# Weight preparation inside the first block of an MLP: bursts against single operations at five places of a round

## The chip, the cores and the metric

The kernel runs on one core of one Trainium2 chip. The metric is the device time of one execution in microseconds (us); lower is better. Five engines matter: PE (TensorE, matmuls), DVE (VectorE), ACT (ScalarE), POOL (GpSimd, nearly unused here) and SP, which issues all DMAs from one queue, in order.

## The reference, cut to what matters

Attention with two kinds of mask gives 2304 tokens of 512 values. Two MLPs follow, one after the other, each with its own `w_in` (512 x 2048) and `w_out` (2048 x 512):

```python
x = attention(q, k, v)                      # 2304 x 512
h = x @ w1_in;  x = relu(h)**2 @ w1_out     # first MLP
h = x @ w2_in;  g = h * sigmoid(1.702 * h)  # second MLP
out = g @ w2_out
```

The inputs are 64-bit floats. Only the preparation of `w2_out`, late in the kernel, is touched here.

## The kernel before, in words

**Number format.** A 64-bit weight is decoded to a 32-bit one by integer operations (`decode_ops`, L140 to L160), and each 32-bit operand is then split into a rounded part and a rest (`wh`, `wl`), so that each product is made of several matmuls.

**The second MLP multiplies by Strassen's scheme.** Each pair of 128-wide slices of the hidden dimension is a pair `p` (0 to 7), and for each pair and each of the two weight matrices seven combinations of the quarter matrices are prepared once, and written to the DRAM tiles `w2d` and `wo2d`. `decode2(o, p)` (L564 to L600) is a Python generator that prepares one pair: an absolute value on ACT (L571), four integer operations on DVE (L146, L148, L153, L157), the sums and differences of quarters on DVE (L582; three for `w_out`), the rounding on ACT (L594, 1792 columns), the rest on DVE (L596, 1792 columns), and two stores of 896 KB on SP (L599). Between any two of these it yields, so that the caller decides where in the instruction order each operation goes. `fill(dve, act)` (L752) draws operations until a budget of estimated microseconds on DVE or ACT is used up. A step may also yield nothing: a pair is begun only two steps of the counter `now` after its raw weights were fetched, and its rounding only two steps after the pair before was finished. Most of the 16 preparations are drawn during the first MLP; at the start of the second MLP the last two pairs of `w_out` (pairs 6 and 7) remain. They are staged in the free tiles `misc[3]` (`wh`) and `misc[4]` (`wl`), where the earlier ones used `wst`.

**The block of the second MLP.** There are three blocks (`i`) of 768 tokens, each with eight rounds (`p`), one for each pair, and then an output stage (L1037 on). A round does seven products (`product`, L669, six matmuls at L673 each) in this order on PE: product 2, product 3, product 6 of the round before, product 4, products 0 and 1 of the next round, product 5. Product 5 adds to the bank X, so it waits until ACT has copied X away (`s3`, L853). On ACT this copy stands behind a sigmoid of the round before (L453), which waits for a DVE addition of the round before (`add`, L845, in `rest`, L994). DVE also multiplies by the sigmoids (L456) and in odd rounds from 3 on forms two sums (`sums`, L866, L848). The order on PE, DVE and ACT is the order of the program (`manual_schedule`); the order of SP's DMAs is made by the planner, which puts a DMA where it expects its operands to be ready, often far ahead of its place in the program. A product's weights are fetched two rounds ahead, into the buffer that the product of this round has just left (`stream`, L656).

**Where the remaining work is drawn.** In rounds 0 to 4 of block 0, `fill(1.8, 1.8)` stands between the DVE multiplication L955 and the addition of `rest`; in round 5, `fill(99, 99)` drains what is left. Then `stream_out(0)` (L875) asks for the first output weights: one load of 1 MB into `misc[5]` for pairs 0 to 3, and one for each of pairs 4 to 7. In round 7 `stream_out(1)` asks for the second set. Each output step `mm_out` (L896) is 18 matmuls at L904.

Of the kernel before, what the change touches and what calls it, by code (L numbers as in the profile page):

```python
# [10 lines left out]
F32R = mybir.dt.float32r  # L11
# [11 lines left out]
def kernel(  # L23
# [20 lines left out]
    nc = tc.nc  # L44
# [519 lines left out]
    def decode2(o, p):  # L564
        while (o, p) not in raw or now[0] < raw[o, p][1] + 2:
            yield None
        place, _ = raw.pop((o, p))
        s, t = stages[place], tmp()
        t2 = t[:, 0:4].rearrange("p x n -> p (x n)")
        s = s.rearrange("p x n -> p (x n)").bitcast(I32).rearrange("p (n two) -> p n two", two=2)  # L570
        nc.scalar.activation(t2, s[:, :, 1].bitcast(F32), AF.Abs)  # L571
        yield "A", 1.06
        for c, _ in zip((0.7, 0.7, 1.2, 1.2), decode_ops(s, t2, False)):
            yield "D", c
        fetch2(place)
        if o:

            forms = ((slice(4, 7, 2), slice(1, 4, 2), slice(0, 2)), (5, 3, 4), (1, 2, 5))
        else:
            forms = ((5, 0, 2), (2, 2, 3), (4, 2, 0), (6, 1, 4))  # L580
        for to, a, b in forms:
            nc.vector.tensor_tensor(  # L582
                out=t[:, to], in0=t[:, a], in1=t[:, b], op=ALU.add if (o, to) == (0, 2) else ALU.subtract)
            yield "D", 0.69 if isinstance(to, slice) else 0.43
        while late and not misc:
            yield None
        if late:
            wh, wl = (misc[n][:, 0:7 * 2 * P].bitcast(F32R).rearrange("p (j n) -> p j n", j=7) for n in (3, 4))
        else:
            w = wstage()  # L590
            wh, wl = w[:, :, 0], w[:, :, 1]
        while now[0] < now[1] + 2:
            yield None
        nc.scalar.copy(wh, t)  # L594
        yield "A", 1.68
        nc.vector.tensor_tensor(out=wl, in0=t, in1=f32(wh), op=ALU.subtract)  # L596
        yield "D", 1.97
        for x, w in enumerate((wh, wl)):
            nc.sync.dma_start(wo2d[:, :, p, x] if o else w2d[:, p, :, x], f32(w))  # L599
        now[1] = now[0]  # L600
# [271 lines left out]
    JS = ((0, "X"), (1, "Z"), (0, "X"), (2, "Y"), (4, "X"), (1, "Y"), (3, "X"))  # L872
    LAST = 4 * len(JS) - 1

    def stream_out(j):  # L875
        if j % 2 == 0:
            src = wo2d[:, WOSEL[j], 0:4].rearrange("p a h n -> p (a h n)")
            nc.sync.dma_start(f32(misc[5]), src)
        for p in range(4 if j % 2 == 0 else 0, NP):
            src, (w, *parts) = wo2d[:, WOSEL[j], p], wx[j % 2][p]  # L880
            if w is not None:
                nc.sync.dma_start(f32(w), src)
            else:
                for h, w in enumerate(parts):
                    nc.sync.dma_start(f32(w), src[:, h])

    def makeop(q):
        j, c = divmod(q, 4)
# [52 lines left out]
    for i in range(N2):  # L941

        waiting, third = iter(()), lambda: None
        for p in range(NP):
            n, c, x = i * NP + p, p // 2, p % 2
            now[0] += 1
            product(n, 2, X, start=False)
            next(waiting, None)
            add(s1, Z[:, 0:NH])
            t = sig(s1, "gh")  # L950
            next(waiting, None)
            s2 = copied(X, 2 + p % 2)
            Y = bank("h")
            product(n, 3, Y)
            times(gf[c][0][:, x], s1, t)  # L955
            if c and x:
                sums(gf[c - 1])
            if i == 0 and p < 6:
                fill(*(1.8, 1.8) if p < 5 else (99, 99))
            if p == 5:  # L960
                stream_out(0)
            if p > 5:
                makeop(p - 6)
            third()
            if p + 1 == NP:
                stream_out(1)
            product(n, 4, X, start=False)
            next(waiting, None)
            s3 = copied(X, 4)
            if p + 1 < NP:  # L970
                Xn = first(n + 1)
                Z = bank("acc")
                product(n + 1, 1, Z)
            else:
                Zo, Xo = ([bank("acc") for _ in range(2)] for _ in range(2))
                mm_out(0, Xo)
            add(s3, Y[:, 0:NH])
            if p + 1 < NP:
                s1 = copied(Xn, (p + 1) % 2)
            next(waiting, None)  # L980
            t = sig(s3, "gh")
            times(gf[c][3][:, x], s3, t)
            product(n, 5, X, start=False)
            def third(n=n, Y=Y):
                product(n, 6, Y, start=False)

            def rest(c=c, x=x, s2=s2, X=X, Y=Y):
                g = gf[c]
                t = lpool.tile([P, NH], F32, tag="tx", name="tx", bufs=1)
                sigmoid(X[:, 0:NH], t)  # L990
                yield
                times(g[1][:, x], X[:, 0:NH], t)
                yield
                add(s2, Y[:, 0:NH])  # L994
                t = sig(s2, "gh")
                yield
                times(g[2][:, x], s2, t)

            waiting = rest()
            X = Xn  # L1000


        more = i + 1 < N2
        if more:
            raw_x = wstage().rearrange("p j h n -> p (j h n)")[:, 0:KC * 2 * NH]
            wst.clear()
            extra = make_x(load_raw(i + 1, f32(raw_x).rearrange("p (c n) -> p c n", c=KC)))
        st = ring(2, [2, 3, 2 * P], F32, "so")
        st2 = tmp()[:, 0:6].rearrange("p (a m) n -> p a m n", a=2)
        ps = {"X": Xo, "Z": Zo, "Y": None}  # L1010
        next(waiting)
        next(waiting)
        makeop(2)
        mm_out(1, Xo)
        third()

        def evac(j):
            if j == 0:
                moved(ps["X"], st[:, 0], nc.scalar.copy)
            elif j == 1:  # L1020
                moved(ps["Z"], st[:, 0], add)
                store(i, 0, 0, st[:, 0])
            elif j == 2:
                moved(ps["X"], st2[:, 0], nc.scalar.copy)
            elif j == 3:
                moved(ps["Y"], st[:, 1], nc.scalar.copy)
            elif j == 4:
                moved(ps["X"], st[:, 1], add)
                store(i, 1, 1, st[:, 1])
            elif j == 5:  # L1030
                moved(ps["Y"], st2[:, 0], add)
                store(i, 0, 1, st2[:, 0])
            else:
                moved(ps["X"], st2[:, 1], nc.scalar.copy)
                store(i, 1, 0, st2[:, 1])

        for q in range(1, LAST + 1):  # L1037
            j, c = divmod(q, 4)
            if q < LAST - 1:
                makeop(q + 2)  # L1040
            if q == 12:
                ps["Y"] = [bank("h") for _ in range(2)]
            if q == LAST and more:
                X = first((i + 1) * NP)
            if q > 1 and (q < LAST or more):
                mm_out(q, ps[JS[j][1]])
            if c == 0:
                evac(j - 1)
            if q == 1:
                next(waiting, None)  # L1050
                next(waiting, None)
            if q == 2:
                sums(gf[3])
            if 3 <= q < 7:
                g = gf[q - 3]
                sub2(g[0], g[2], g[0])
            elif q > 6:
                next(extra, None)
                if q in (9, 11, 13, 15):
                    g = gf[(q - 9) // 2]  # L1060
                    sub2(g[1], g[1], g[0])
            if c == 3 and j + 2 < len(JS):
                stream_out(j + 2)
            if q == 24 and more:
                for _ in extra:
                    pass
                stream((i + 1) * NP)
                stream((i + 1) * NP + 1)
        if more:
            Z = bank("acc")  # L1070
            product((i + 1) * NP, 1, Z)
            hs = ring(2, [5, NH], F32, "hs")
            s1 = copied(X, 0)
            evac(6)
        else:
            mm_out(LAST, ps["X"], (2,))
            nc.vector.tensor_copy(st2[:, 1, 2], ps["X"][1][:, 0:2 * P])
            store(i, 1, 0, st2[:, 1], slice(2, 3))
            mm_out(LAST, ps["X"], (0, 1))
            nc.scalar.copy(st2[:, 1, 0], ps["X"][0][:, 0:2 * P])  # L1080
            nc.vector.tensor_copy(st2[:, 1, 1], ps["X"][0][:, 2 * P:4 * P])
            store(i, 1, 0, st2[:, 1], slice(0, 2))
# [45 lines left out]
```

## Time and profile before

| | us |
|---|---|
| median of 3 runs (884.33 to 886.2) | 884.43 |
| the profiled execution, its own time | 884.62 |
| its span in the trace | 882.8 |
| start of product 4 of round 0 to the first output matmul, block 0 (516.33 to 577.66) | 61.33 |
| the same stretch of block 1 (644.36 to 696.88) | 52.52 |

The profile is of one execution, and every time in it counts from the start of the span. The profiled execution's time is 1.82 us more than its span (what lies around the span), and 0.19 us above the median. Engine times overlap, so busy shares don't add up. A row of the timeline merges neighbouring instructions of one kind: start, length, engine, line, operation, tiles written and read, shape, count, and in brackets the idle time before it with the engine and line that ended it. A product of six matmuls takes 1.05 us from its start to that of the next; the last matmul's modelled end lies some 0.16 us behind that.

### The profile page before, as it was taken

The page shows a single profiled execution, that of the slowest core. Times are in us where ns is not written, and L with a number is a line of the kernel's source. Part 1 is how long each engine was busy: PE and PEld are TensorE (multiplying, and loading weights), DVE is VectorE, ACT ScalarE, POOL GpSimd, SP SyncE. Part 2 cuts the span into 40 slices and gives each one's busy share as a digit, 9 for nine tenths or more (in the row PEclk, how much of TensorE's full clock was granted, in tenths as well). Part 3 has the DMA queues.
Part 4 walks back from the last instruction along what each step waited for, and adds up shares of the span by engine and source line. Part 5 has one row for each costly group of instructions (what it writes and reads, how often), then busy time and mean ns, then how long its engine had stood idle before and what let it go on. Part 6 is the DMA issues. An engine that isn't in the chain of part 4 may idle for free.

```text
span 882.8 us, 15997 instructions
## 1 busy us (share of the span) xinstructions
PE 863.1 (98%) x5851; PEld 771.0 (87%) x5857; DVE 613.9 (70%) x1315; ACT 492.7 (56%) x1160; POOL 2.6 (0%) x12
## 2 busy tenths in 40 slices
PE   8899999999999999999999998899999999999998
PEld 5578788888889998888877898899999999999998
DVE  5999996545546645788868767688646798357863
ACT  7988895544536645555646644455444555344542
POOL 0000000000000000000000000000000000000000
PEclk9999999999999999999999999999999999999999
DMA  8997210211114205887999499978898497986673
GB/s 203 302 324 227 65 34 28 88 39 47 34 34 113 46 2 188 267 266 267 311 334 297 136 334 368 310 258 280 271 371 251 161 340 258 334 286 206 200 249 109
DMA packets 146129, 181.85 MB, mean 206 GB/s; under 512 B 41508, under 2 KB 101124, under 8 KB 144516
## 3 DMA queue, kind: packets, MB, share of 16 engines
q1 hardware_dynamic: 146052, 180.84, 62.7%
q8 instruction: 47, 0.77, 0.4%
q14 instruction: 30, 0.25, 0.1%
HBM read 142.00 MB, written 38.80 MB: 205 GB/s over the span
## 4 chain that ended last, share of the span: by engine, by line
PE 68%; DVE 16%; ACT 6%; issue 4%; DMA 3%; SPq 1%; ACTq 0%; DVEq 0%
PE ps_acc L904 15%; PE ps_acc L476 12%; PE ps_h L414 11%; PE ps_att L673 10%; PE ps_h L904 6%; PE ps_h L673 5%; DVE tmp L153 3%; DVE tmp L157 3%; PE ps_acc L673 2%; DMA stg<-in_moe_w_out_dram 2%; DVE tmp L146 2%; ACT tmp L571 2%; DVE tmp L582 1%; PE ps_h L366 1%; DVE tmp L148 1%
## 5 line engine op out<-in xcount | busy, mean ns | idle before, releaser
L414 PE MATMUL ps_h<-xr,whl 128*128 128x512 f32 (+1 forms) x948 | 210.3, 371 | 0.0
L414 PEld LDWEIGHTS ps_h<-xr,whl 128*128 128x128 f32 x948 | 164.6, 188 | 30.5
L476 PE MATMUL ps_acc<-gh,whl 128*128 128x512 f32 (+1 forms) x640 | 148.8, 375 | 1.1 <-ACT gh L444 1.1
L476 PEld LDWEIGHTS ps_acc<-gh,whl 128*128 128x128 f32 x640 | 110.2, 188 | 21.1 <-ACT gh L444 2.1
L317 ACT ACTIVATE pr<-pr,st 72x72 f32<-72x72 f32 (+1 forms) x224 | 81.2, 368 | 18.3 <-DVE st L303 18.2
L476 PE MATMUL ps_acc<-gl,whl 128*128 128x512 f32 (+1 forms) x320 | 79.0, 369 | 0.8 <-DVE gl L449 0.8
L453 ACT ACTIVATE gh<-hs 128x384 f32<-128x384 f32 x72 | 37.7, 524 | 62.3 <-DVE hs L845 62.3
L476 PEld LDWEIGHTS ps_acc<-gl,whl 128*128 128x128 f32 x320 | 56.7, 189 | 11.5 <-DVE gl L449 1.4
L443 ACT ACTIVATE t<-ps_h 128x512 f32<-128x512 f32 (+1 forms) x64 | 34.4, 538 | 56.7 <-PE ps_h L414 44.0
L673 PE MATMUL ps_att<-xop,wst 128*128 128x384 f32 x288 | 59.0, 339 | 5.0 <-ACT hs L853 5.0
L673 PE MATMUL ps_att<-xop 128*128 128x384 f32 x288 | 59.0, 339 | 1.4 <-ACT hs L853 1.4
L673 PEld LDWEIGHTS ps_att<-xop,wst 128*128 128x128 f32 x288 | 51.1, 188 | 5.6 <-ACT hs L853 5.6
L904 PE MATMUL ps_acc<-misc,gop 128*128 128x256 f32 x432 | 54.2, 283 | 0.0
L890 ACT CAST gop<-misc 128x768 fp32r<-128x768 f32 x42 | 34.7, 833 | 34.6 <-PE ps_acc L904 19.0
L890 ACT CAST gop<-g 128x768 fp32r<-128x768 f32 x42 | 34.8, 834 | 34.1 <-PE ps_acc L904 18.4
L673 PEld LDWEIGHTS ps_att<-xop 128*128 128x128 f32 x288 | 51.3, 191 | 2.2 <-ACT hs L853 2.0
L904 PEld LDWEIGHTS ps_acc<-misc,gop 128*128 128x128 f32 x432 | 53.2, 191 | 0.0
L845 DVE TENSOR_TENSOR hs<-ps_h,hs 128x384 f32<-128x384 f32 x49 | 27.2, 555 | 35.9 <-ACT hs L853 25.1
L848 DVE TENSOR_TENSOR gop<-g,gop 128x768 fp32r<-128x768 f32 x42 | 40.2, 956 | 16.9 <-ACT gop L890 16.9
L449 DVE TENSOR_TENSOR gl<-t,gh 128x512 fp32r<-128x512 f32 (+1 forms) x64 | 39.8, 622 | 17.2 <-ACT t L446 16.3
L594 ACT CAST wst<-tmp 128x1792 fp32r<-128x1792 f32 x14 | 23.7, 1696 | 49.5 <-DVE tmp L582 43.0
L848 DVE TENSOR_TENSOR gop<-misc,gop 128x768 fp32r<-128x768 f32 x42 | 39.9, 957 | 13.8 <-ACT gop L890 13.7
(131 smaller groups left out, 1472.6 us busy)
## 6 DMA issues: line engine op xcount, KB each, us to landing
xop<-w2d SPq DMA_DIRECT2D x84, 256.0 KB
wst<-w2d SPq DMA_DIRECT2D x84, 256.0 KB
xop<-wo2d SPq DMA_DIRECT2D x63, 256.0 KB
w2d<-wst SPq DMA_DIRECT2D x16, 896.0 KB
misc<-wo2d SPq DMA_DIRECT2D x12, 1024.0 KB
wo2d<-wst SPq DMA_DIRECT2D x12, 896.0 KB
wx<-wo2d SPq DMA_DIRECT2D x36, 256.0 KB
stg<-in_moe_w_in_dram SPq DMA_DIRECT2D x16, 512.0 KB
```

The lines of the kernel that those rows point to most:

```text
L153: nc.vector.scalar_tensor_tensor(out=ti, in0=low, scalar=29, in1=ti, op0=ALU.logical_shift_right, op1=ALU.bitwise_or,)
L317: nc.scalar.activation(pr[0:R, i, j, 0:N], pr[0:R, i, j, 0:N], AF.Exp, bias=st[0:R, 0, x:x + 1], scale=-1.0, accum_out=st[0:R, 1, x:x + 1],)
L414: nc.tensor.matmul(ph[:, 0:nb], w[:, kk * P:(kk + 1) * P], x[:, kk], start=(kk == KS[0] and w is ih and x is xh), stop=(kk == KS[-1] and x ...
L443: nc.scalar.activation(t, ph[:, 0:nb], AF.Relu)
L449: nc.vector.tensor_tensor(out=gl, in0=t, in1=f32(gh), op=ALU.subtract)
L453: nc.scalar.activation(t, h, AF.Sigmoid, scale=1.702)
L476: nc.tensor.matmul(acc[c][:, 0:nb], w[:, c * P:(c + 1) * P], x, start=(f == 0 and w is oh and not lo), stop=(f == NF - 1 and lo == 1),)
L673: nc.tensor.matmul(ps[:, 0:NH], w[:, a, k * P:(k + 1) * P], x[:, b + k], start=start and y == 0, stop=y == len(prods) - 1, skip_group_chec ...
L845: nc.vector.tensor_tensor(out=h, in0=ps, in1=h, op=ALU.add)
L848: nc.vector.tensor_tensor(out=out, in0=a, in1=b, op=op)
L890: nc.scalar.copy(hi, g)
L904: nc.tensor.matmul(part(ps, m), g, w[1 + h], start=j in (0, 1, 3) and p == 0 and m != 1 and not last and h == 0, stop=p == NP - 1 and last ...
```

## The change

In the last two preparations (`late`), the rounding goes to `misc[4]` and the rest is written in place, over `t`, so that `misc[3]` is not used. Rounding and rest are each done in two pieces, of columns 0 to 1023 and 1024 to 1791, all roundings first. `fill` is gone from the rounds of the second MLP. A new function `more` draws one step of the generator; in block 0 it is called at five places of rounds 0, 1, 2, 4 and 6, and at the last two of them in rounds 3, 5 and 7. What is then left is drained in round 7. `stream_out(0)` is asked for in round 6 for pairs 0 to 5 and in round 7 for pairs 6 and 7, in all three blocks. (The old variable `more` is renamed `going`; these lines are left out below.)

```diff
         if late:
-            wh, wl = (misc[n][:, 0:7 * 2 * P].bitcast(F32R).rearrange("p (j n) -> p j n", j=7) for n in (3, 4))
+            wh, wl = misc[4][:, 0:7 * 2 * P].bitcast(F32R).rearrange("p (j n) -> p j n", j=7), t.bitcast(F32R)
...
-        nc.scalar.copy(wh, t)
-        yield "A", 1.68
-        nc.vector.tensor_tensor(out=wl, in0=t, in1=f32(wh), op=ALU.subtract)
-        yield "D", 1.97
+        parts = (slice(0, 4), slice(4, 7)) if late else (slice(0, 7),)
+        for x in parts:
+            nc.scalar.copy(wh[:, x], t[:, x])
+            yield "A", 1.68
+        for x in parts:
+            nc.vector.tensor_tensor(out=wl[:, x], in0=t[:, x], in1=f32(wh)[:, x], op=ALU.subtract)
+            yield "D", 1.97
...
-    def stream_out(j):
-        if j % 2 == 0:
-            src = wo2d[:, WOSEL[j], 0:4].rearrange("p a h n -> p (a h n)")
-            nc.sync.dma_start(f32(misc[5]), src)
-        for p in range(4 if j % 2 == 0 else 0, NP):
+    def stream_out(j, ps=range(NP)):
+        for p in ps:
             src, (w, *parts) = wo2d[:, WOSEL[j], p], wx[j % 2][p]
-            if w is not None:
+            if j % 2 == 0 and p < 4:
+                if p == 0:
+                    nc.sync.dma_start(f32(misc[5]), wo2d[:, WOSEL[j], 0:4].rearrange("p a h n -> p (a h n)"))
+            elif w is not None:
                 nc.sync.dma_start(f32(w), src)
...
+    def more(i, p, last=False):
+        if i == 0 and (last or p < 3 or p % 2 == 0):
+            next(extra, None)
...
             add(s1, Z[:, 0:NH])
             t = sig(s1, "gh")
+            more(i, p)
...
             times(gf[c][0][:, x], s1, t)
             if c and x:
                 sums(gf[c - 1])
-            if i == 0 and p < 6:
-                fill(*(1.8, 1.8) if p < 5 else (99, 99))
-            if p == 5:
-                stream_out(0)
+            more(i, p)
+            if p == 6:
+                stream_out(0, range(6))
             if p > 5:
                 makeop(p - 6)
             third()
             if p + 1 == NP:
+                for _ in extra:
+                    pass
+                stream_out(0, range(6, NP))
                 stream_out(1)
...
             s3 = copied(X, 4)
+            more(i, p)
...
             add(s3, Y[:, 0:NH])
             if p + 1 < NP:
                 s1 = copied(Xn, (p + 1) % 2)
+            more(i, p, True)
             next(waiting, None)
             t = sig(s3, "gh")
             times(gf[c][3][:, x], s3, t)
+            more(i, p, True)
             product(n, 5, X, start=False)
```

## Rows read from the trace of the kernel before

**Rows 1.** The page's first part: busy time, share and instructions of each engine.

```profile
PE 863.1 (98%) x5851; PEld 771.0 (87%) x5857; DVE 613.9 (70%) x1315; ACT 492.7 (56%) x1160; POOL 2.6 (0%) x12
```

**Rows 2.** Windows: stretch, length; busy PE, PEld, DVE, ACT, POOL; clock, DMA share, GB/s.

```profile
516.33:577.66 61.33, 54.99 (x302) 54.03 (x302) 45.41 (x72) 28.03 (x53) 0.00 (x0) 0.97 0.97 343
644.36:696.88 52.52, 52.52 (x302) 52.52 (x302) 31.19 (x55) 23.34 (x50) 0.00 (x0) 1.00 0.81 272
```

**Rows 3.** Timeline of PE in block 0, the products around the stalls.

```profile
533.25 1.22 PE L673 MATMUL ps_acc<-xop,wst 128*128 128x384 f32 x6
535.84 1.32 PE L673 MATMUL ps_att<-xop 128*128 128x384 f32 x6 [1.36 <-ACT hs L853]
...
542.22 1.20 PE L673 MATMUL ps_acc<-xop 128*128 128x384 f32 x6
545.17 1.56 PE L673 MATMUL ps_att<-xop,wst 128*128 128x384 f32 x6 [1.75 <-ACT hs L853]
546.52 2.12 PE L673 MATMUL ps_att<-xop 128*128 128x384 f32 x6
548.44 1.70 PE L673 MATMUL ps_h<-xop 128*128 128x384 f32 x6
...
560.51 1.21 PE L673 MATMUL ps_acc<-xop 128*128 128x384 f32 x6
564.95 1.31 PE L673 MATMUL ps_att<-xop,wst 128*128 128x384 f32 x6 [3.23 <-ACT hs L853]
```

**Rows 4.** Windows of 2 us, columns as in rows 2.

```profile
524.00:526.00 2.00, 2.00 (x13) 2.00 (x13) 0.98 (x3) 0.89 (x2) 0.00 (x0) 1.00 1.06 406
546.50:548.50 2.00, 2.00 (x8) 2.00 (x8) 1.86 (x5) 1.01 (x2) 0.00 (x0) 0.50 1.06 396
580.00:582.00 2.00, 2.00 (x16) 2.00 (x15) 1.41 (x3) 1.47 (x3) 0.00 (x0) 1.00 0.00 0
```

**Rows 5.** Timeline of DVE, rounds 2, 3 and 5 of block 0.

```profile
529.67 0.88 DVE L582 TENSOR_TENSOR tmp<-tmp 128x256 f32<-128x256 f32 x2
532.31 2.03 DVE L596 TENSOR_TENSOR misc<-tmp,misc 128x1792 fp32r<-128x1792 f32 x1 [1.76 <-ACT misc L594]
...
539.12 1.95 DVE L848 TENSOR_TENSOR g<-g 128x768 f32<-128x768 f32 x2
...
542.44 1.23 DVE L153 SCALAR_TENSOR_TENSOR tmp<-stage,tmp 128x1024 int32<-128x1024 int32 x1
...
548.45 1.22 DVE L157 SCALAR_TENSOR_TENSOR tmp<-stage,tmp 128x1024 int32<-128x1024 int32 x1
549.71 0.69 DVE L582 TENSOR_TENSOR tmp<-tmp 128x512 f32<-128x512 f32 x1
...
556.92 1.95 DVE L848 TENSOR_TENSOR g<-g 128x768 f32<-128x768 f32 x2
...
561.42 2.02 DVE L596 TENSOR_TENSOR misc<-tmp,misc 128x1792 fp32r<-128x1792 f32 x1 [1.76 <-ACT misc L594]
```

**Rows 6.** Timeline of ACT, rounds 2 and 3 of block 0.

```profile
530.58 1.69 ACT L594 CAST misc<-tmp 128x1792 fp32r<-128x1792 f32 x1 [0.85 <-DVE tmp L582]
534.90 0.52 ACT L453 ACTIVATE gh<-hs 128x384 f32<-128x384 f32 x1 [2.62 <-DVE hs L845]
535.33 0.84 ACT L853 COPY hs<-ps_att 128x384 f32<-128x384 f32 x2
...
538.88 1.16 ACT L571 ACTIVATE tmp<-stage 128x1024 f32<-128x1024 f32 x1
```

**Rows 7.** One line's instructions (L633, L635): duration in ns, least, median, most.

```profile
L633 ACT CAST xop<-xraw x4: 820/829/838, 483.9 to 502.9; 128x768 fp32r<-128x768 f32 x4
L635 DVE TENSOR_TENSOR xop<-tmp,xop x9: 950/953/960, 491.5 to 748.2; 128x768 fp32r<-128x768 f32 x9
```

**Rows 8.** Timeline of SP's queue in block 0.

```profile
526.37 0.97 SPq L124 DMA_DIRECT2D stage<-in_moe_w_out_dram  x2
...
553.72 0.42 SPq L878 DMA_DIRECT2D misc<-wo2d  x1
```

More of the change, by code (lines that the diff above doesn't have):

```diff
@@ L1000 @@
             X = Xn
-        more = i + 1 < N2
-        if more:
+        going = i + 1 < N2
+        if going:
             raw_x = wstage().rearrange("p j h n -> p (j h n)")[:, 0:KC * 2 * NH]
@@ L1042 @@
                 ps["Y"] = [bank("h") for _ in range(2)]
-            if q == LAST and more:
+            if q == LAST and going:
                 X = first((i + 1) * NP)
-            if q > 1 and (q < LAST or more):
+            if q > 1 and (q < LAST or going):
                 mm_out(q, ps[JS[j][1]])
@@ L1063 @@
                 stream_out(j + 2)
-            if q == 24 and more:
+            if q == 24 and going:
                 for _ in extra:
@@ L1068 @@
                 stream((i + 1) * NP + 1)
-        if more:
+        if going:
             Z = bank("acc")
```

## The prediction

> **What bounds the kernel now.** I read the page's busy line first: PE works 98% of the span and DVE 70% [rows 1]. So a change that lays DVE and ACT work elsewhere can win only where PE stands still, and the question is where those 2% lie. The second view is the pair of windows over the same 50 products in two blocks [rows 2]: block 1 needs 52.52 us with PE busy all through, block 0 needs 61.33. Block 0 differs in that it also prepares the last two weight pairs; the reader sees DVE busy 45.41 us there against 31.19. The difference, 61.33 - 52.52 = **8.81 us, is the most that this change can win**, about 1% of 884.62.
>
> The third view, PE's timeline, shows where the 8.81 us are [rows 3]. Three products start late, all of them product 5, all released by ACT's copy at L853. A product follows the last by 1.05 us, so product 5 of round 2 was due at 534.30 and came at 535.84 (1.54 late), that of round 3 at 543.27 and came at 545.17 (1.90), that of round 5 at 561.56 and came at 564.95 (3.39): 6.83 us. After the second stall three products are slow (1.56, 2.12 and 1.70 busy where 1.21 is usual: 1.75 us more) because the granted clock fell to 0.50, which is 1.2 instead of 2.4 GHz [rows 4]. 6.83 + 1.75 = 8.6; the rest is pipeline refill.
>
> The fourth view is the two engines behind the copy. In round 2 ACT waits 2.62 us for the DVE addition L845, then does the sigmoid, then the copy that PE needs [rows 6]; DVE cannot add because `fill` has put 4.67 us ahead of it (529.67 to 534.34: two differences, a wait of 1.76 for the rounding, and the rest L596) [rows 5]. So DVE work between L955 and the addition is free up to some slack and beyond it costs one for one. The slack, three times: round 2, 4.67 - 1.54 = 3.1; round 5, from the sums at 556.92 to 563.44, 6.52 - 3.39 = 3.1; round 3, sums and three integer operations, 539.12 to 543.67, 4.55 - 1.90 = 2.65 [rows 3, 5].
>
> **The change, part by part.** *One operation at each place.* Stepping the generator through the calls: round 0 draws L146, L148, L153, L157 and the first difference; round 1 two differences, both roundings and the first rest; round 2 the second rest, then the stores, L571, L146, L148, L153; round 3 (two places) L157 and a difference; round 4 two differences, both roundings, the first rest; round 5 the second rest; after that nothing is left. The two conditions on `now` (raw weights two steps old, pair before two steps done) are met with no step to spare in rounds 2 and 4. Ahead of the critical addition now stand at most, in one round, 0.88 us (rounds 1 and 4), 0.95 (round 2) or the sums of 1.95 (rounds 3 and 5) [rows 5, 7], all under the 2.65 of slack. By this count all three stalls go: -6.83.
>
> *What carries over.* The other places lie before the same queues of the next round. Round 3's DVE has seven operations of its own at some 0.48, 3.4 us, the sums 1.95, L157 1.22 and 0.69 for a difference [rows 5], 7.2 of the 7.35 us that seven products take, so what is late there stays late. I stepped the three in-order queues through the eight rounds with these durations. For the kernel before this gives stalls of 1.4, 1.7 and 3.3 us (shown: 1.36, 1.75, 3.23 [rows 3]); for the changed order 0.4 (product 4 of round 4, its copy late behind a late addition), 0.6 (product 4 of round 5: the sigmoid of round 4 stands behind the two rounding pieces on ACT, and the rest piece behind that) and 0.3 (product 5 of round 5). Moving each duration by 5% moves the sum between 0.3 and 2.3. I take **+1.3**.
>
> *The pieces.* A rounding of 768 columns takes 0.83, one of 1792 takes 1.69 [rows 6, 7]: on a line through both, 1024 take 1.05, so two pieces cost 0.19 more, and the rest (0.95 against 2.03 [rows 5, 7], so 1.22 for 1024) 0.14 more. Twice each, 0.7 us of ACT and DVE time, contained in the walk; uncovered it would cost those 0.7.
>
> *The clock.* It fell once, right after gaps of 1.36 and 1.75 us some ten us apart [rows 3, 4]; the lone 3.23 us at 564.95 left the next products at 1.2 busy. With gaps of at most 0.6 I take no fall: -1.75; bounds 0 and -1.75.
>
> The Trainium skill speaks against this: TensorE: Matmul & The Clock Gate, section "A second HAM failure mode: psum-queue depth-cycling", tells of a kernel whose PE paused briefly but often between groups of matmuls, and whose clock swung between its two levels. By that rule the clock's 1.75 us would stay lost; the trace agrees so far only for the larger gaps above.
>
> *In place, and `misc[3]`.* The rest over `t` has the same shape, hence the same time. Its buffer is needed again only in the output stage, after the store; `misc[4]` is next written by the sums of round 7, some 15 us after the last rounding. Cost nothing; without that cover, one store of 0.9 MB, 2.3 us at the 396 GB/s [rows 4].
>
> *The DMAs.* L571 of pair 7 comes about 9 us earlier, its raw weights (issued at 526.37 [rows 8], once L157 of pair 6 is through) can be asked for some 3 us earlier by the walk. If they land late, ACT waits at a place with 2.65 us of slack: 0, at worst 1. The stores follow L596 and block SP's queue for what is left of it, at both ends of the change alike. `stream_out(0)` is asked for a round later, but SP issued its 1 MB load at 553.72, in round 4, ahead of its place in round 5 [rows 8], and what needs it starts at 577.66 now, 570 after: 0, bounds below.
>
> **Sum.** 884.62 - 8.81 + 1.3 = **877.1 us**, against the profiled execution. The median is 0.19 lower, less than the uncertainty of any term. After the rounds PE runs without a gap (2.00 of 2.00 us at 580 to 582 [rows 4]), so the gain stays.
>
> **Rivals.** *The clock falls again* on small gaps: 877.1 + 1.75 = 878.9. For it: two gaps of 0.4 and 0.6 seven us apart; against it: only gaps above 1.3 are followed by a fall in the trace.
>
> *DMA becomes the bound.* The stretch moves 343 GB/s over 61.33 us, 21.0 MB, with a share of 0.97; the fastest rows show 396 and 406 at a share of 1.06 [rows 2, 4]. In 53.8 us the same bytes would be 391 GB/s, the limit. Against it: some 2 MB of them are loads that PE reads only after the stretch, DMA stands idle at 580 to 582 [rows 4], and weights are asked for two rounds (14.7 us) ahead. If weights of rounds 2 to 5 come late, about half of the 6.83 us returns as waits on DMA: 880.5.
>
> *The output weights come late, and the kernel is slower.* Place: the first output matmul, waiting for the 1 MB into `misc[5]`. If the planner puts this load at its new place behind the second set's loads, it goes out near 571 with 2.6 MB ahead of it, 3.7 MB in all: at 396 GB/s it lands near 580.3, 10.1 after 570.2, and the time is 877.1 + 10.1 = 887.2. It costs from 570.2 on, and the kernel is slower from a landing at about 577.7. For it: the program order moved that way, and the planner decides by its own reckoning. Against it: before, the load was two rounds ahead of its users.
>
> *The change doesn't do what it says.* If one of the conditions on `now` misses its step, the generator slips and round 7 drains a rounding and a rest in one piece, with the stores and pair 7's load behind them: stalls like round 5's 3.39 plus a second of 3 to 4, some 883.5 to 884, no difference.
>
> **How the numbers follow.** A measurement of this kernel can tell about 0.2% (1.8 us) from no change. Chances: forecast 0.62 (875.8 to 878.2), clock 0.13, DMA 0.15, slippage 0.05, output weights late 0.05. Faster by over 0.2%: 0.62 + 0.13 + 0.15 = 0.90; within: 0.05; slower: 0.05. The range starts at 875.6, where all 8.81 us are won, and ends at 880.5, the price of the DMA case; left out are half of that case and the last two, under 0.2.
>
> **What would show it.** In the changed profile: block 0's stretch takes 53 to 55 us; no PE gap above 0.7 us in rounds 2, 3 and 5; granted clock 1.00 throughout; small gaps in rounds 4 and 5, released by L853. Rounding pieces of 1.05 and 0.83, rest pieces of 1.22 and 0.95. The forecast is wrong if PE's gaps there are released by a DMA, if the first output matmul waits for `misc[5]`, or if L594 still appears in round 6 or 7.

## The result, and the profile after

The changed kernel's median is **877.9 us** (876.94 to 879.25, 4 runs) against 885.32 (884.33 to 887.23, 4 runs) for the kernel before; the ratio is 0.9915, with a 95% interval of 0.9891 to 0.9939. The forecast was 877.1 and the range 875.6 to 880.5.

The profiled execution took 876.94 us with a span of 875.1. The stretch from product 4 of round 0 to the first output matmul now reads as follows (windows; length, busy PE, PEld, DVE, ACT, POOL, clock, DMA share, GB/s).

```profile
515.72:569.88 54.16, 53.68 (x301) 52.37 (x301) 43.38 (x73) 27.65 (x55) 0.00 (x0) 1.00 1.04 378
```

It is 54.16 us long where it was 61.33 [rows 2], so 7.17 us are gone from it, and the granted clock is 1.00 throughout (0.97 before). DVE does the same work in it, but for the pieces and for one L146 of 0.69 us that now falls just ahead of it (at 514.66). What follows the stretch took 305.2 us (875.1 - 569.88) where it took 305.1 (882.8 - 577.66). What precedes it was 0.61 us shorter, though but for that L146 nothing was changed there: it lies within the scatter of the kernel's start. That is the whole difference of the two spans: 7.17 + 0.61 - 0.1 = 7.7.

The next view is PE's timeline: the four products that started late in rounds 2, 4 and 5, each with the one before it. Counted from 1.05 us behind that one, they are 0.13, 0.42, 0.25 and 0.29 us late, in place of 1.54, 1.90 and 3.39 [rows 3].

```profile
529.47 1.22 PE L676 MATMUL ps_h<-xop,wst 128*128 128x384 f32 x6
530.65 1.31 PE L676 MATMUL ps_att<-xop 128*128 128x384 f32 x6
...
544.42 1.22 PE L676 MATMUL ps_h<-xop,wst 128*128 128x384 f32 x6
545.89 1.31 PE L676 MATMUL ps_att<-xop 128*128 128x384 f32 x6 [0.25 <-ACT hs L856]
...
552.32 1.20 PE L676 MATMUL ps_h<-xop 128*128 128x384 f32 x6
553.62 1.32 PE L676 MATMUL ps_att<-xop,wst 128*128 128x384 f32 x6
554.78 1.20 PE L676 MATMUL ps_att<-xop 128*128 128x384 f32 x6
555.82 1.21 PE L676 MATMUL ps_acc<-xop 128*128 128x384 f32 x6
557.16 1.32 PE L676 MATMUL ps_att<-xop,wst 128*128 128x384 f32 x6
```

DVE's timeline of rounds 3 to 5 shows what is late now. Behind the sums (L851, formerly L848) and an addition DVE idles 1.02 us. From 541.15 on L157 and a difference stand in one row of work with the kernel's own operations, ahead of the addition at 544.30. In the next round the first rest (550.90) stands ahead of the addition at 552.03.

```profile
537.72 1.95 DVE L851 TENSOR_TENSOR g<-g 128x768 f32<-128x768 f32 x2
...
541.15 0.56 DVE L848 TENSOR_TENSOR hs<-ps_h,hs 128x384 f32<-128x384 f32 x1 [1.02 <-ACT hs L856]
541.63 1.22 DVE L157 SCALAR_TENSOR_TENSOR tmp<-stage,tmp 128x1024 int32<-128x1024 int32 x1
...
543.70 0.68 DVE L582 TENSOR_TENSOR tmp<-tmp 128x512 f32<-128x512 f32 x1
544.30 0.55 DVE L848 TENSOR_TENSOR hs<-ps_acc,hs 128x384 f32<-128x384 f32 x1
...
550.90 1.22 DVE L599 TENSOR_TENSOR tmp<-tmp,misc 128x1024 fp32r<-128x1024 f32 x1
552.03 0.55 DVE L848 TENSOR_TENSOR hs<-ps_acc,hs 128x384 f32<-128x384 f32 x1
...
557.62 0.95 DVE L599 TENSOR_TENSOR tmp<-tmp,misc 128x768 fp32r<-128x768 f32 x1
```

ACT's timeline of rounds 4 and 5 shows the two sigmoids that wait for these additions; the copies that product 4 of rounds 4 and 5 waits for stand right behind them. Between them lie the two rounding pieces, on both sides of a copy, in place of the 1.69 us of rows 6, and a sigmoid of round 4 behind them (549.85).

```profile
544.95 0.52 ACT L453 ACTIVATE gh<-hs 128x384 f32<-128x384 f32 x1 [1.92 <-DVE hs L848]
...
547.80 1.05 ACT L596 CAST misc<-tmp 128x1024 fp32r<-128x1024 f32 x1
548.75 0.48 ACT L856 COPY hs<-ps_att 128x384 f32<-128x384 f32 x1
549.12 0.85 ACT L596 CAST misc<-tmp 128x768 fp32r<-128x768 f32 x1
549.85 0.54 ACT L453 ACTIVATE gh<-hs 128x384 f32<-128x384 f32 x1
...
552.68 0.52 ACT L453 ACTIVATE gh<-hs 128x384 f32<-128x384 f32 x1 [1.79 <-DVE hs L848]
```

SP's queue asked for the raw weights 3.8 us earlier than before (3.2 counted from the start of the stretch), and for the 1 MB of output weights at almost the same time as before [rows 8], though the program now asks for them a round later.

```profile
522.60 1.53 SPq L124 DMA_DIRECT2D stage<-in_moe_w_out_dram  x2
...
552.82 1.31 SPq L883 DMA_DIRECT2D misc<-wo2d  x1
```

### The profile page after: what moved, and what is told of

The parts are those of the page before. It is cut to its first block, busy times and chain, and to the rows that moved or that the text cites. A ratio compares the mean times of both kernels' runs of the same rounds, so it can differ in the third digit from the quotient of the medians.

```text
span 875.1 us, 16005 instructions
## 1 busy us (share of the span) xinstructions
PE 861.2 (98%) x5857; PEld 768.9 (88%) x5857; DVE 612.7 (70%) x1317; ACT 492.0 (56%) x1162; POOL 2.6 (0%) x12
## 4 chain that ended last, share of the span: by engine, by line
PE 76%; DVE 9%; DMA 7%; ACT 3%; SPq 2%; issue 2%; ACTq 0%; DVEq 0%
PE ps_acc L476 18%; PE ps_h L414 17%; PE ps_acc L912 15%; PE ps_att L676 9%; PE ps_h L912 6%; PE ps_h L676 5%; PE ps_acc L676 2%; DMA stg<-in_moe_w_out_dram 2%; DMA stage<-in_moe_w_out_dram 2%; PE ps_h L366 1%; PE ps_att L287 1%; SPq L245 1%; DVE tmp L153 1%; DVE tmp L157 1%; PE ps_att L341 1%
## 5 line engine op out<-in xcount | busy, mean ns | idle before, releaser
L414 PE MATMUL ps_h<-xr,whl 128*128 128x512 f32 (+1 forms) x948 | 210.7, 371 | 0.7 <-DVE whl L183 0.7
L414 PEld LDWEIGHTS ps_h<-xr,whl 128*128 128x128 f32 x948 | 164.6, 188 | 31.6 <-DVE whl L183 1.2
L848 DVE TENSOR_TENSOR hs<-ps_h,hs 128x384 f32<-128x384 f32 x49 | 27.2, 556 | 35.7 <-ACT hs L856 24.8
L851 DVE TENSOR_TENSOR gop<-g,gop 128x768 fp32r<-128x768 f32 x42 | 40.2, 957 | 16.9 <-ACT gop L898 16.9
L851 DVE TENSOR_TENSOR gop<-misc,gop 128x768 fp32r<-128x768 f32 x42 | 39.9, 957 | 13.8 <-ACT gop L898 13.7
```

Of the source, the lines that this page charges most:

```text
L414: nc.tensor.matmul(ph[:, 0:nb], w[:, kk * P:(kk + 1) * P], x[:, kk], start=(kk == KS[0] and w is ih and x is xh), stop=(kk == KS[-1] and x ...
L848: nc.vector.tensor_tensor(out=h, in0=ps, in1=h, op=ALU.add)
L851: nc.vector.tensor_tensor(out=out, in0=a, in1=b, op=op)
```

## The experiments

A late product is given below by how much later than 1.05 us after its predecessor it started; where the clock is full, the product behind it starts 0.1 later too. The stretch is the one of the table above.

### One piece at the five places

```diff
-        parts = (slice(0, 4), slice(4, 7)) if late else (slice(0, 7),)
+        parts = (slice(0, 7),)
```

> The changed kernel, but rounding and rest in one piece of 1792 columns each, drawn at the same places. Theory (the stalls were DVE work queued ahead of the addition of L994, beyond some 2.7 us of slack; where an operation is put matters, not its length): stepping the queues gives one gap, 1.4 us before product 4 of round 2, and the gaps of rounds 4 and 5 gone, 1.5 us in all against the 1.6 of the changed kernel. Stretch from product 4 of round 0 to the first output matmul 53.5 to 54.5 us, time 877.2 to 878.4, no difference from the changed kernel. Rival (shorter pieces are what removed the stalls): gaps of over 1.5 us come back in both preparations, 3 us or more, 881 or above.

Median 878.11 us (4 runs), ratio to the kernel before 0.9928 (0.9912 to 0.9945); stretch 54.56. One product is late, product 4 of round 2, by 1.65; rounds 4 and 5 have none. The timelines of PE, then of DVE, then of ACT around it in this kernel:

```profile
530.92 1.22 PE L676 MATMUL ps_h<-xop,wst 128*128 128x384 f32 x6
533.62 1.32 PE L676 MATMUL ps_att<-xop 128*128 128x384 f32 x6 [1.48 <-ACT hs L856]
```

DVE, the rest of pair 6:

```profile
528.00 2.02 DVE L599 TENSOR_TENSOR tmp<-tmp,misc 128x1792 fp32r<-128x1792 f32 x1 [1.03 <-ACT misc L596]
```

ACT, the absolute value of pair 7 and the copy that ends PE's idle time:

```profile
532.08 1.12 ACT L571 ACTIVATE tmp<-stage 128x1024 f32<-128x1024 f32 x1
533.10 0.47 ACT L856 COPY hs<-ps_att 128x384 f32<-128x384 f32 x1
```

The 2 us rest makes the next round's addition and sigmoid late, and L571, which this order draws one place earlier, stands right ahead of the copy that PE waits for. So shorter pieces are not what removed the stalls; without them the stretch is 0.4 longer than in the changed kernel, and the medians (878.11 and 877.9) don't tell the two apart.

### The pieces in the old bursts

The kernel before, with the changed kernel's staging and pieces, and this in place of `fill`:

```diff
-                fill(*(1.8, 1.8) if p < 5 else (99, 99))
+                for _ in range((3, 2, 6, 4, 2, 99)[p]):
+                    next(extra, None)
```

> The kernel before, with the two pieces and the rest in place, but drawn in the same bursts at the same place as before (3, 2, 6, 4, 2 steps in rounds 0 to 4, what is left in round 5). Theory: the three gaps before product 5 stay, a little smaller because the second rounding runs beside the first rest: 0.6, 1.5 and 2.5 us by the stepped queues, stretch 57.4 us, or 59.2 if the clock falls too; time 881 to 883. Rival (shorter pieces are what removed the stalls): stretch under 55.5, time under 879.3.

Median 884.54 us (10 runs), ratio to before 0.9990 (0.9978 to 1.0003), no difference; stretch 59.99. The three products that were late before are late again, by 0.96, 1.84 and 2.81, in this kernel's timeline of PE:

```profile
536.04 1.32 PE L676 MATMUL ps_att<-xop 128*128 128x384 f32 x6 [0.79 <-ACT hs L856]
...
545.36 1.31 PE L676 MATMUL ps_att<-xop,wst 128*128 128x384 f32 x6 [1.69 <-ACT hs L856]
...
562.97 2.29 PE L676 MATMUL ps_att<-xop,wst 128*128 128x384 f32 x6 [2.65 <-ACT hs L856]
```

The products are each 0.3 us later than I stepped out, and the clock fell behind the last one (2.29 us for that product), so the time lies above the 881 to 883 that I gave. The rival fails: short pieces drawn in a burst, with the rest in place, save 0.6, 0.1 and 0.6 us of the three gaps, and no more.

### The old bursts at the end of the round

The kernel before, unsplit; `fill` (and `stream_out(0)`) moved behind the last multiplication of the round:

```diff
             times(gf[c][3][:, x], s3, t)
+            if i == 0 and p < 6:
+                fill(*(1.8, 1.8) if p < 5 else (99, 99))
+            if p == 5:
+                stream_out(0)
             product(n, 5, X, start=False)
```

> The kernel before, its bursts unsplit, but drawn at the end of each round (after the last DVE multiplication) and no longer ahead of the addition of L994. Theory (each place has its own slack, and a burst of over 4 us exceeds all of them): the gaps move from product 5 to product 4 of the next round, by the stepped queues 0.3, 2.2, 1.8 and 3.0 us in rounds 1, 3, 4 and 6, 8 us in all: stretch 60.5, to 62.5 if the clock falls; time 884 to 886.5, no better than before. Rival (only work ahead of that one addition hurts, at any other place it is free): stretch under 55.5, time under 879.3.

Median 888.13 us (5 runs), ratio 1.0041 (1.0024 to 1.0058): slower than before by 0.4%; stretch 63.64. Product 5 is no longer the late one; product 4 is, in rounds 1, 3, 4 and 6, by 0.52, 2.51, 0.88 and 3.48 (timeline of PE):

```profile
526.20 1.32 PE L673 MATMUL ps_att<-xop,wst 128*128 128x384 f32 x6 [0.37 <-ACT hs L853]
...
543.52 1.74 PE L673 MATMUL ps_att<-xop,wst 128*128 128x384 f32 x6 [2.35 <-ACT hs L853]
...
553.39 1.33 PE L673 MATMUL ps_att<-xop 128*128 128x384 f32 x6 [0.71 <-ACT hs L853]
...
571.98 2.29 PE L673 MATMUL ps_att<-xop 128*128 128x384 f32 x6 [3.31 <-ACT hs L853]
```

The gaps moved where the stepped queues put them; round 4's came out smaller (0.88 for 1.8), and the clock fell twice where I had allowed for one fall, hence most of the miss on the time. Taking the work away from ahead of the one addition is not enough: a burst exceeds the slack at the other end of the round too.

### Other places for single operations

`more` with a table of places instead of its rule. The five places of a round are called a to e, in the order of the program, and each call names its own (those lines are left out):

```diff
-    def more(i, p, last=False):
-
-        if i == 0 and (last or p < 3 or p % 2 == 0):
+    DRAW = ("abde", "acd", "abce", "bde", "abcde", "bde", "ab", "")
+
+    def more(i, p, place):
+        if i == 0 and place in DRAW[p]:
             next(extra, None)
```

> The changed kernel with other places for single operations, chosen by stepping the queues so that no gap is left: places a, b, d, e of round 0; a, c, d of 1; a, b, c, e of 2; b, d, e of 3; all five of 4; b, d, e of 5; a, b of 6. Theory (what is left of the gaps is queue order on ACT and DVE too): stretch 52.5 to 53.2 us, the 52.52 of the blocks without preparation; 1 to 1.6 us less than the changed kernel, 876.3 to 877. Rival (what is left is DMA, weights that come late): stretch stays at 54 or more, time 877.5 to 878.5, with gaps released by a DMA.

Median 877.28 us (5 runs), ratio to before 0.9923 (0.9908 to 0.9938); the stretch is 52.84, PE busy in all of it (windows, columns as in rows 2):

```profile
516.42:569.26 52.84, 52.84 (x302) 52.54 (x302) 42.99 (x73) 27.65 (x55) 0.00 (x0) 1.00 1.05 387
```

The theory holds: what the changed kernel leaves is queue order on ACT and DVE. The stretch lies in the range that I gave, the median 0.3 us above it. The same row speaks against DMA as the next bound: 387 GB/s at a share of 1.05, and no product is late by more than 0.1. Behind the stretch this kernel took 305.4 us (874.7 - 569.26) where the changed one took 305.2: it gives 0.2 back at the first product after the first output step.

### The slack measured by itself

The changed kernel, with operations of known length ahead of the critical addition in blocks 1 and 2, where nothing else is prepared:

```diff
+        if i:
+            dm = tmp().rearrange("p x n -> p (x n)")[:, 0:2 * NH].rearrange("p (x n) -> p x n", x=2)
...
+            for _ in range({(1, 2): 4, (1, 4): 6, (2, 2): 5, (2, 4): 8}.get((i, p), 0)):
+                sub2(dm, gf[0][0], gf[0][0])
```

> The changed kernel with DVE subtractions of 768 columns (0.87 us each) added ahead of the addition of L994, in four rounds of the blocks that prepare nothing; their results are not used. Block 1: 4 in round 2 and 6 in round 4; block 2: 5 in round 2 and 8 in round 4. Theory (work there is free up to a slack of some 3 us, then costs one for one): product 5 late by 0.2 (4 ops, 3.5 us), 1.05 (5, 4.35), 1.9 (6, 5.2) and 3.7 (8, 7.0); about 7 us in all, up to 1.75 more wherever the clock falls behind a gap. Rival (the engines are only 60% busy there, so the work fits in): no product late by over 0.3.

One execution, 890.22 us. PE's timeline with the four late products:

```profile
654.96 1.32 PE L676 MATMUL ps_att<-xop 128*128 128x384 f32 x6 [0.64 <-ACT hs L856]
...
672.56 1.34 PE L676 MATMUL ps_att<-xop 128*128 128x384 f32 x6 [2.62 <-ACT hs L856]
...
780.52 1.33 PE L676 MATMUL ps_att<-xop 128*128 128x384 f32 x6 [1.63 <-ACT hs L856]
...
800.11 2.29 PE L676 MATMUL ps_att<-xop 128*128 128x384 f32 x6 [4.60 <-ACT hs L856]
```

DVE's timeline with six of the operations:

```profile
665.14 5.92 DVE L851 TENSOR_TENSOR tmp<-g 128x768 f32<-128x768 f32 x6
```

4, 6, 5 and 8 operations make the product 0.81, 2.79, 1.80 and 4.78 late. One operation takes 0.99 us in such a row (5.92 / 6), not the 0.87 I had put in, so each of my numbers was too small. Work minus lateness is 3.96 - 0.81 = 3.15, 4.95 - 1.80 = 3.15, 5.94 - 2.79 = 3.15 and 7.92 - 4.78 = 3.14: the slack is **3.15 us** in these even rounds, and every microsecond beyond it is a microsecond of PE. Behind the two largest gaps the clock fell on top of that (2.29 us for the product at 800.11, 2.10 for the one behind 672.56 where 1.21 is usual); behind 0.64 and 1.63 it did not.

### Gaps and the clock

> As e5_slack, with other rounds: block 1: 6 subtractions in round 2 and 4 in round 3; block 2: 5, 5, 3, 5, 3, 4 in rounds 1 to 6. Stepping the queues gives gaps of 1.9 and 2.4 in two neighbouring rounds of block 1, and six of 1.0 to 1.5 in block 2. Theory (only large gaps bring the clock down): granted clock under 1.00 behind block 1's pair, 1.00 in block 2. Rival (many small pauses bring it down as well, as the Trainium skill tells in TensorE: Matmul & The Clock Gate, section A second HAM failure mode: psum-queue depth-cycling): granted clock under 1.00 in block 2 again and again, and products of over 1.3 us there.

The same edit with the other table: `{(1, 2): 6, (1, 3): 4, (2, 1): 5, (2, 2): 5, (2, 3): 3, (2, 4): 5, (2, 5): 3, (2, 6): 4}`. One execution, 898.24 us. PE's idle times before the late products were 2.62 and 1.43 us in block 1, and 1.75, 2.10, 0.43, 2.08, 1.95 and 1.96 in block 2. Two of the late products in PE's timeline:

```profile
803.57 1.34 PE L676 MATMUL ps_att<-xop 128*128 128x384 f32 x6 [2.08 <-ACT hs L856]
...
822.74 2.24 PE L676 MATMUL ps_att<-xop 128*128 128x384 f32 x6 [1.96 <-ACT hs L856]
```

Windows behind five of the gaps (the clock is the third number from the end):

```profile
657.50:663.00 5.50, 5.50 (x23) 5.50 (x24) 5.15 (x9) 2.31 (x5) 0.00 (x0) 0.69 0.35 98
...
784.00:790.00 6.00, 5.73 (x24) 5.73 (x25) 5.40 (x9) 2.63 (x6) 0.00 (x0) 0.72 0.40 115
...
803.00:806.00 3.00, 2.44 (x14) 2.44 (x15) 2.33 (x5) 2.10 (x6) 0.00 (x0) 1.00 0.27 91
812.00:816.00 4.00, 2.85 (x16) 2.85 (x17) 2.67 (x7) 2.88 (x7) 0.00 (x0) 1.00 0.45 133
822.00:827.00 5.00, 4.26 (x15) 4.26 (x16) 3.51 (x7) 2.80 (x7) 0.00 (x0) 0.66 0.18 49
```

The clock fell behind the gaps of 2.62, 2.10 and 1.96, and not behind those of 1.43, 1.75, 0.43, 2.08 and 1.95. Block 2's gaps came out larger than planned, so my expectation of 1.00 there was not put to the test that it was meant for; the second fall in block 2, behind a gap of 1.96 after three that were followed by none (0.43, 2.08, 1.95), is not explained by the gap's length.

### The first output weights asked for last

```diff
-            if p == 6:
-                stream_out(0, range(6))
...
-                stream_out(0, range(6, NP))
+                stream_out(0)
```

> The changed kernel, but with all first output weights asked for in round 7; SP's order then has the 1 MB load into misc[5] three DMAs ahead of the last one of the rounds, instead of behind the stores of round 4. Theory (hidden as long as it is issued some 5 us ahead): issued near 567.5, it lands near 572, the first output matmul waits 2 to 3 us for it, time 879 to 881.5. Rival (loads are hidden wherever they are asked for): first output matmul follows without a gap, 877 to 878.5.

One execution, 879.2 us. Now the load does go out later; SP's timeline:

```profile
564.02 0.50 SPq L883 DMA_DIRECT2D misc<-wo2d  x1
```

PE's timeline, the last product and the first output matmul:

```profile
569.53 1.22 PE L676 MATMUL ps_att<-xop,wst 128*128 128x384 f32 x6
572.03 2.42 PE L912 MATMUL ps_acc<-misc,gop 128*128 128x256 f32 x18 [1.28 <-DMA misc<-wo2d]
```

It was issued 3.5 us earlier than I had reckoned and took 8.0 us to the matmul (572.03 - 564.02); the wait is 1.28 us instead of 2 to 3. The theory holds in kind: the request in round 6 costs nothing because it still goes out at 552.82, and asked for wholly in round 7 it costs 1.3 us. The rival, that loads are hidden wherever they are asked for, falls by this wait; the time of one execution would not settle it.

### One piece, other places

The kernel of the fourth experiment with `parts = (slice(0, 7),)` and the places below.

```diff
+    DRAW = ("abe", "abcde", "ab", "acde", "cd", "ace", "ab", "")
```

> The changed kernel with rounding and rest in one piece of 1792 columns each, at places chosen by stepping the queues: a, b, e of round 0; all five of 1; a, b of 2; a, c, d, e of 3; c, d of 4; a, c, e of 5; a, b of 6, so that the rounding stands at the end of a round and the rest at the beginning of the next. Theory (place matters, length doesn't): no gap, stretch 52.5 to 53.2 us, as e4_other_places. Rival (one piece of 2 us can't be hidden anywhere): a gap of 1 us or more in rounds 1 to 2 and 5 to 6, stretch over 54.5.

The stretch is 52.65 us, without a late product. The rounding stands behind the last sigmoid of round 1 and the rest behind the first addition of round 2. ACT's timeline:

```profile
529.99 1.68 ACT L596 CAST misc<-tmp 128x1792 fp32r<-128x1792 f32 x1
```

DVE's timeline:

```profile
531.70 2.03 DVE L599 TENSOR_TENSOR tmp<-tmp,misc 128x1792 fp32r<-128x1792 f32 x1 [0.43 <-ACT misc L596]
```

So length does not matter where the place has room. The median is 877.85 us all the same (875.87 to 878.93, 6 runs): in the profiled execution the stretch began at 519.29 instead of 515.72, and these 3.6 us arise in the first 45 us. PE waits there for a load of `q`, and behind that wait the granted clock is 0.58 over 4 us, where it is 1.00 in the changed kernel's trace. PE's timeline, then a window (columns as in rows 2):

```profile
38.48 0.47 PE L266 MATMUL ps_att<-ident,ld 72*128 72x72 f32 x4 [1.63 <-DMA ld<-in_q_dram]
```

```profile
40.00:44.00 4.00, 4.00 (x29) 2.86 (x28) 1.92 (x5) 0.50 (x2) 0.00 (x0) 0.58 1.06 317
```

The matmuls at L414 right behind the wait start 2.3 us later than in the changed kernel (39.39 for 37.09), and the work behind the clock's fall 3.8 us later (L341 at 43.49 for 39.69). The scatter between the six runs fits this: the three with a mean granted clock of 1.00 took 875.87 to 877.06, the three with 0.997 or 0.998 took 878.64 to 878.93. Where the clock fell in the runs without a trace is not known.

### The changed kernel and the best places, side by side

> The changed kernel as it is, on one chip with e10_other_places_again. Its stretch was 54.16 us, that of e4_other_places 52.84, and what follows the stretch took the same in every trace so far; the first 50 us differ by 1 to 3 us between executions. Theory: stretch 54.2 again, median 1.3 us above e10_other_places_again. Rival (the gaps differ from execution to execution): stretch off by over 0.5.

> The kernel of e4_other_places again, beside e9_changed_again on one chip. Theory: stretch 52.8 and a median 1.3 us under e9_changed_again, so that it is the fastest of all. Rival (its gain is lost elsewhere): a median within 0.4.

The changed kernel again: median 877.63 (877.34 to 878.85, 5 runs), stretch 54.18. The fourth experiment's kernel again: median 877.3 (875.9 to 879.26, 5 runs), stretch 52.80. The stretches repeat to 0.04, and differ by 1.38; the profiled executions differ by 1.44 (877.34 and 875.9). The medians differ by only 0.33, within the 0.4 of the rival, so the 1.3 that I expected of them did not show. Some of it is lost behind the stretch (305.4 us for 305.2, as in the fourth experiment); for the rest, the start of the kernel scatters by more than what is to be measured: the stretch began between 515.48 and 519.29 us in the traces of kernels with the single operations. That the other places save 1.3 to 1.4 us in the stretch is shown; that the kernel as a whole is faster than the changed one is likely, and these runs don't settle it.

## Why the prediction was right, point by point

**The ceiling.** 8.81 us lay in the stretch of block 0; the change took 7.17 and the fourth experiment 8.49 (61.33 - 52.84). Behind the stretch the change won or lost nothing (305.2 for 305.1).

**The cause of the stalls** holds: DVE work queued ahead of the addition, beyond a slack. The slack read from three rows was 3.1, 3.1 and 2.65; measured by itself it is 3.15. Round 3's 2.65 was too small since DVE came late into that round: its row of work began 4.15 us before the product was due (539.12 to 543.27), those of rounds 2 and 5 began 4.63 and 4.64 before. No run draws single operations with `stream_out(0)` left in round 5; that its later place plays no part rests on the traces, where ACT's copy ends PE's gaps and the load leaves at almost the same time.

**That the place counts, and the length little**, was in the sum only as arithmetic; the pieces in the old bursts (no gain), one piece at the five places (nearly all of it) and one piece at other places (no gap) show it. The pieces took 1.05, 0.85, 1.22 and 0.95 us, as interpolated.

**What carries over** was put at 1.3, as gaps of 0.4, 0.6 and 0.3. It is 0.42, 0.25 and 0.29, at the products named, with 0.13 in round 2 that I had not named, and 0.1 behind each late product and behind the first of the stretch that I had left out: 54.16 - 52.52 = 1.64. DVE was less full in round 3 than the 7.2 of 7.35 us that I had added up: it idled 1.02 us before 541.15, for ACT's copy. The mis-sized term is product 4 of round 5 (0.25 for 0.6); its cause, the rounding pieces and the rest in round 4, is in the rows above.

**The clock** stayed at 1.00, so its 1.75 us are won: four products late by 0.13 to 0.42 us within 27 us brought no fall here, while two of the six gaps of 1.4 to 2.1 us in the sixth experiment did. By the rule of the Trainium skill's page TensorE: Matmul & The Clock Gate, section "A second HAM failure mode: psum-queue depth-cycling", where a kernel's many short pauses make its clock swing, the 1.75 us would have stayed lost; for pauses as small as these the trace does not agree.

**DMA as the bound** did not come: I had put the limit at 391 GB/s for the whole stretch, and 378 and 387 were moved without a product waiting for a DMA (20.5 MB in the stretch, not the 21.0 that I had put in). **Late output weights** did not come either; the seventh experiment made them late, and the price was 1.3 us, not the 10.1 of the rival, since the load went out at 564 and not near 571, among the second set's loads and not behind all of them. **Slippage** did not come: the last rest ends at 558.57, in round 5.

The 0.8 us between forecast and median is partly the 0.34 us (1.64 - 1.3) of the carried term; the rest is within the scatter of the kernel's start. That the profiled execution came within 0.16 us of the forecast (876.94) is luck: the 0.61 us that its start happened to be shorter outweighs those 0.34.

## What to carry to other kernels

Work that is to be hidden in a pipelined loop has a slack for each place in each engine's queue, and it can be read: the work between two points minus the lateness of the product that waits, from rows with a stall; here three rows gave 2.65 to 3.1 where 3.15 was measured. Draw the work one operation at a time, and count for each place what stands ahead of the next instruction that the bottleneck waits for; splitting operations is worth little once their place is right. When the total scatters by more than the effect, compare the stretch between two fixed instructions: it repeated to 0.04 us, where five runs of one kernel spread over 1.5 to 3.4 us.

## What the runs showed that I had not expected

The clock does not follow a gap's length alone. In the kernel before, PE idled 3.23 us before 564.95 and stayed at 2.4 GHz; in the second experiment 2.65 us were followed by 1.2 GHz, and in the sixth 1.96 us were, while 2.08 and 1.95 were not. A fall cost 1.5 to 1.75 us of PE's busy time each time, as much as a gap of medium size. What decides between them was not found.

The time at which a DMA goes out does not follow its place in the program step by step: asked for a round later, the 1 MB load left 0.9 us earlier (552.82 against 553.72; 0.3 earlier counted from the start of the stretch); asked for one round later still, it left 11 us later, at 564.02. What the planner goes by is not shown.
